# First mixture: the first of four weight groups multiplied plainly, token differences kept raw for two units

## The chip, the cores and the metric

The kernel runs on one core of one Trainium2 chip. The metric is the device time of one launch in microseconds. Shorter is better; each version is run several times and the median is told. TensorE multiplies into PSUM, ScalarE (ACT) and VectorE (DVE) read PSUM and SBUF, GpSimd (POOL) reads SBUF alone, and SyncE (SP) issues nearly all transfers between SBUF and DRAM.

## What is computed

Retention attention, then a dense mixture ("first mixture"), then a mixture of eight experts whose gate is balanced over tokens and experts ("second mixture"). All of it is float32.

```python
scores = scale * np.matmul(q, k.transpose(0, 1, 3, 2))
attn = np.matmul(scores * Dmat[None], v)               # 4 x 8 heads x 576 x 64
x = attn.transpose(0, 2, 1, 3).reshape(2304, 512)
h = x @ w_in                                           # w_in 512 x 2048: first mixture
x = (h * (1.0 / (1.0 + np.exp(-1.702 * h)))) @ w_out   # w_out 2048 x 512
...                                                    # P: gate of x, eight rounds of row and column sums
for e in range(8):
    out += P[:, e:e + 1] * (np.maximum(x @ w1[e], 0.0) @ w2[e])
```

The factors of the first mixture come in as 64-bit floats, seen as pairs of 32-bit words.

## The kernel before

**Exact products from two parts.** A float32 operand is split into a high part (a copy on ScalarE rounded to the matmul type float32r) and a low part (operand less high part, on VectorE or GpSimd). One product takes three matmuls: high by high, high by low, low by high.

**First mixture.** The 2048 inner columns are four groups of 512 (`G1`), the 2304 tokens three passes of 768 (`NPASS`), two halves `t` of `N` = 384 tokens each. One group and one pass make a unit; there are 12, units 0 to 2 with group 0, units 3 to 5 with group 1, and so on. A unit computes h for the two halves `h` of the group's columns, gates it (`gated`: two steps on ScalarE, then the low part, kept in `lows` until the next matmuls are issued) and multiplies by the group's part of `w_out` (`out_part`), whose result `out_done` copies into `xacc` (group 0, ScalarE) or adds to it (later groups, VectorE). In each half h comes by a scheme of seven products (`unit_step`, 0 to 6) instead of eight: weights AK, AL, BL and the sums S1 to S4, tokens X1K, X1L, X2L and the differences T1 to T4. So operands have to be made: sums of weights on GpSimd, differences of tokens on VectorE, and a high and a low part of each.

**Where the operands live.** `wi[0]` and `wi[1]` hold the seven weight operands of the two halves, `wo[0]` the split part of `w_out`. The tokens of a unit lie in seven of the 12 slots of `ring`; in units 0 to 2 they are made (`token_zero` during attention, `token_unit`) and put to `token_store`, from where `load_token` brings them for later groups. The differences overwrite blocks of `xacc`, the same blocks that `out_done` of the unit fills later.

**Weights.** 64-bit pieces of 128 x 256 arrive by `load_piece`; `read_piece` makes float32 of one in five steps on VectorE and one on ScalarE. Group 0's are joined by `add_piece` and split straight into `wi` by `direct_tasks`. For groups 1 to 3, and for the first two expert weights, `staged_tasks` splits each operand into a small buffer in `wo[1]` (`stage`), one or two of them, puts it to `sub_store` (`first_store`), and `load_sub` loads it into `wi` at the change of groups. `split_out` and `put_out` do the like for `w_out`, `load_out` loads it.

**Order.** All of it is in an order written by hand. After each slot (six matmuls; 30 slots to a unit) `run` issues the side work that `plan` holds for the slot; `place_tasks` spreads a list over a stretch of slots. Every engine, and SP's queue, works through its instructions in that order, and an instruction that waits holds those behind it. During attention (16 pairs of heads and batches) the same is done by `weave`, `settle` and the lists `prep` and `tok`.

Of the kernel before, what the change touches and what calls it, by code (L numbers as in the profile page):

```python
# [21 lines left out]
def retention_moe_kernel(  # L22
# [48 lines left out]
    ring = [keep.tile([P, 7 * 4 * N], F32R, name="ring0")]  # L71
    wi = [keep.tile([P, 14 * QF], F32R, name="wi0")]
# [129 lines left out]

    def split_out(g, i, h):
# [30 lines left out]
    def sums_of(r1, box):  # L234
# [19 lines left out]
        def src(o):  # L254
            if o in (S1, S3, S2, S4):
                return box["s"][:, (o - S1) % 2]
            return half(*{AK: (0, 0), AL: (0, 1), BL: (1, 1)}[o])

        return sums, src, half

    def direct_tasks(r1, w):


        box = {}
        sums, src, half = sums_of(r1, box)

        def whole(what):
# [1728 lines left out]
```

## Time and profile before

| what | us |
|---|---|
| median of 3 runs | 2004.01 (2003.08 to 2008.91) |
| the profiled execution, its time | 1998.25 |
| its span, first to last instruction | 1996.5 |
| attention ends, unit 0 begins | 84.58 |
| first mixture, units 0 to 11 | 464.77 |
| second mixture begins | 549.35 |
| TensorE busy | 1915.4 (96%) |
| VectorE, GpSimd, ScalarE busy | 1470.8, 1337.4, 749.8 |

The times of the middle rows are places in the profiled execution; the unit boundaries are the first matmul of each unit. A busy TensorE is one with a matmul in its pipe; where it was held, the idle time before an instruction is told with what ended it.

### The profile page before, as it was taken

Reading aid. Unit: us, or ns where it says so; the run is one execution under the profiler, and the core shown is the slowest. Engines: PE = TensorE matmul, PEld = TensorE weight load, DVE = VectorE, ACT = ScalarE, POOL = GpSimd, SP = SyncE. Lnnn points to the kernel's source line nnn. Section 1 sums busy time; section 2 is a strip of 40 time slices with the busy share of each in tenths; the row PEclk is TensorE's granted clock in tenths of the full one; section 3 lists DMA queues with packets and bytes.
Section 4 is the critical chain, followed back from the end, with each engine's and each line's share of the span. In section 5 each row is a group of like instructions: output and inputs, shape, how many; then the busy total and the mean of one; then the engine's idle time right before and its main releaser. Section 6 shows DMA issues by size and latency. Waiting matters only on the chain.

```text
span 1996.5 us, 33594 instructions
## 1 busy us (share of the span) xinstructions
PE 1915.4 (96%) x11431; PEld 1833.4 (92%) x11431; DVE 1470.8 (74%) x2454; ACT 749.8 (38%) x1600; POOL 1337.4 (67%) x1347
## 2 busy tenths in 40 slices
PE   9687798999999999999999999999999999999998
PEld 7577797888989889999999999999999999999998
DVE  6866456664678777777666888888777887777788
ACT  4544333334345444444443322222224222222462
POOL 5765233332168888888866777777777777777777
PEclk9989999999999999999999999999999999999999
DMA  9278968787368888888888777877778788777774
GB/s 392 103 290 307 337 233 288 287 290 295 133 239 300 296 300 301 297 310 316 303 294 272 254 272 247 272 254 260 261 255 269 255 288 263 258 261 253 270 245 169
DMA packets 246025, 538.42 MB, mean 270 GB/s; under 512 B 35168, under 2 KB 89184, under 8 KB 245088
## 3 DMA queue, kind: packets, MB, share of 16 engines
q1 hardware_dynamic: 232208, 534.62, 76.7%
q10 hardware_dynamic: 13648, 1.67, 0.5%
q8 instruction: 91, 1.49, 0.3%
q14 instruction: 78, 0.64, 0.1%
HBM read 380.15 MB, written 156.06 MB: 269 GB/s over the span
## 4 chain that ended last, share of the span: by engine, by line
PE 72%; DMA 10%; DVE 7%; POOL 5%; issue 3%; ACT 2%; SPq 0%; POOLq 0%; DVEq 0%; ACTq 0%
PE ps_p L1707 20%; PE ps_y L1337 13%; PE ps_z L1337 9%; PE ps_x L1337 9%; PE ps_m L1367 8%; PE ps_m L1261 4%; DMA sub<-wo 4%; PE ps_p L1719 3%; DMA second<-mix 2%; DMA r<-in_w_dram 1%; PE ps_y L1191 1%; DVE acc L1382 1%; DMA wo<-out 1%; PE ps_x L1191 1%; PE ps_z L1191 1%
## 5 line engine op out<-in xcount | busy, mean ns | idle before, releaser
L1731 DVE TENSOR_TENSOR acc<-ps_p,acc 128x768 f32<-128x768 f32 x420 | 399.9, 952 | 114.6 <-PE ps_p L1707 104.6
L1707 PE MATMUL ps_p<-wo,wi 128*128 128x384 f32 x2352 | 470.9, 334 | 0.1
L1707 PEld LDWEIGHTS ps_p<-wo,wi 128*128 128x128 f32 x2352 | 413.1, 188 | 0.8 <-issue 0.6
L1337 PE MATMUL ps_y<-ring,wi 128*128 128x384 f32 x1728 | 342.2, 335 | 0.0
L1590 POOL TENSOR_TENSOR wo<-u,wo 128x384 fp32r<-128x384 f32 x190 | 194.4, 1023 | 180.8 <-ACT wo L1589 180.8
L1337 PEld LDWEIGHTS ps_y<-ring,wi 128*128 128x128 f32 x1728 | 302.9, 188 | 3.4 <-issue 0.5
L1367 PE MATMUL ps_m<-wo,wo 128*128 128x512 f32 x1152 | 269.5, 391 | 0.2 <-DVE acc L1378 0.2
L1367 PEld LDWEIGHTS ps_m<-wo,wo 128*128 128x128 f32 x1152 | 215.0, 188 | 44.3 <-DVE acc L1382 0.7
L1589 ACT ACTIVATE wo<-u 128x384 fp32r<-128x384 f32 x191 | 100.4, 526 | 390.0 <-POOL u L1593 255.0
L1337 PE MATMUL ps_z<-ring,wi 128*128 128x384 f32 x1152 | 231.6, 335 | 2.5 <-DVE wo L1351 2.5
L1337 PE MATMUL ps_x<-ring,wi 128*128 128x384 f32 x1152 | 230.7, 334 | 0.0
L1337 PEld LDWEIGHTS ps_z<-ring,wi 128*128 128x128 f32 x1152 | 201.6, 188 | 4.4 <-DVE wo L1351 4.1
L1337 PEld LDWEIGHTS ps_x<-ring,wi 128*128 128x128 f32 x1152 | 201.9, 188 | 0.0
L1590 POOL TENSOR_TENSOR wo<-r,wo 128x384 fp32r<-128x384 f32 x127 | 132.2, 1041 | 22.8 <-ACT wo L1589 22.4
L1590 POOL TENSOR_TENSOR wo<-p,wo 128x384 fp32r<-128x384 f32 x127 | 136.3, 1073 | 5.5 <-ACT wo L1589 5.1
L1382 DVE SCALAR_TENSOR_TENSOR acc<-ps_m,pr,acc 128x512 f32<-128x512 f32 x168 | 123.7, 744 | 19.4 <-PE ps_m L1367 19.0
L1261 PE MATMUL ps_m<-g,wo 128*128 128x384 f32 x576 | 112.2, 348 | 22.5 <-DMA wo<-out 10.0
L1261 PEld LDWEIGHTS ps_m<-g,wo 128*128 128x128 f32 x576 | 104.4, 196 | 27.2 <-DMA wo<-out 11.2
L1589 ACT ACTIVATE wo<-p 128x384 fp32r<-128x384 f32 x127 | 65.9, 519 | 146.3 <-POOL p L1593 142.1
L1261 PE MATMUL ps_m<-wo,wo 128*128 128x384 f32 x576 | 104.0, 338 | 4.2 <-DVE acc L1275 4.2
L1261 PEld LDWEIGHTS ps_m<-wo,wo 128*128 128x128 f32 x576 | 101.4, 190 | 5.1 <-DVE acc L1275 5.1
L889 POOL TENSOR_TENSOR wi<-s,wi 128x512 fp32r<-128x512 f32 x60 | 78.4, 1306 | 39.8 <-ACT wi L882 39.2
(203 smaller groups left out, 3189.9 us busy)
## 6 DMA issues: line engine op xcount, KB each, us to landing
wi<-second SPq DMA_DIRECT2D x189, 512.0 KB, 5.1
wi<-first SPq DMA_DIRECT2D x135, 512.0 KB, 5.1
wi<-first SPq DMA_DIRECT2D x192, 256.0 KB, 4.8
ring<-token SPq DMA_DIRECT2D x63, 768.0 KB, 8.3
first<-wi SPq DMA_DIRECT2D x90, 512.0 KB, 3.7
r<-in_w_dram SPq DMA_DIRECT2D x64, 512.0 KB, 5.6
second<-wo SPq DMA_DIRECT2D x32, 512.0 KB, 3.1
second<-wt SPq DMA_DIRECT2D x64, 256.0 KB, 5.3
```

Source lines behind the costliest of these rows:

```text
L889: nc.gpsimd.tensor_tensor(out=wl[:, ks], in0=t[:, ks], in1=r32(wh[:, ks]), op=ALU.subtract)
L1191: nc.tensor.matmul(out=t[:, 0:N], lhsT=ops[:, w, hw, c], rhs=x[:, hx, c], start=begin and c == 0 and i == 0, stop=end and c == 1 and i == ...
L1261: nc.tensor.matmul(out=pd[:, 0:N], lhsT=w_out_of[:, d, hw, f], rhs=gs[t][:, f, hg], start=first and f == fs[0] and k == 0, stop=last and f ...
L1337: nc.tensor.matmul(out=t[:, 0:N], lhsT=w[:, o, hw, c], rhs=xq(q, x, hx, c), start=begin and c == 0 and i == 0, stop=end and c == 1 and i == 2,
L1367: nc.tensor.matmul(out=t, lhsT=x[:, is_], rhs=w[:, h, f], start=f == 0 and k == 0, stop=f == 1 and k == 2,)
L1382: nc.vector.scalar_tensor_tensor(out=oa, in0=tv, scalar=pr[:, ti, e : e + 1], in1=oa, op0=ALU.mult, op1=ALU.add)
L1589: nc.scalar.activation(out=h, in_=src, func=ACTF.Copy)
L1590: eng.tensor_tensor(out=l, in0=src, in1=r32(h), op=ALU.subtract)
L1707: nc.tensor.matmul(out=places[:, j], lhsT=w[:, hw, j * P : (j + 1) * P], rhs=a, start=k == 0, stop=k == 2,)
L1719: nc.tensor.matmul(out=t[:, j * QF : (j + 1) * QF], lhsT=a[:, js], rhs=w[:, hw], start=k == 0, stop=k == 2,)
L1731: nc.vector.tensor_tensor(out=e, in0=done, in1=e, op=ALU.add)
```

## The change

Units 0 to 2 compute h plainly: eight tiles (`h`, block `b`, token half `t`) of 12 matmuls each, on unsplit blocks of weights and tokens, in `plain_unit`. They have 32 slots. For that the eight input pieces of group 0 are split directly into four places of each `wi` (`split_in`), during attention; the tokens are split into four slots of the ring per pass (`plain_hi`, `plain_lo`; pass 0 from PSUM in attention, passes 1 and 2 in the unit before). In these units VectorE still makes the differences in `xacc`, but they are put raw to `diff_store` (`keep_diff`); two units later `load_token` loads one into half a slot, and `split_token` splits it there (two steps on ScalarE, two on GpSimd) and keeps it for groups 2 and 3. The undifferenced operands are kept as they are (`keep_plain_token`), and two stay in place for unit 3.

The staging of input weights goes. Of a later group one half waits as float32 in SBUF and the other in `half_store` (512 KB); in the last unit of the group before, behind its last use of `wi[0]` and of `wi[1]`, both are split directly into `wi` (`direct_tasks`). The first two expert weights are done likewise in unit 11. `put_out` has two buffers in turn. `load_out` moves forward, and the order of the output tiles in units 3 to 11 changes so that the first half of `wo` is done earlier. Token loads get fixed slots of a unit instead of the place behind the last use. In the second mixture two stores of first-layer weights are added and one PSUM bank is taken from another set.

```diff
-    ring = [keep.tile([P, 7 * 4 * N], F32R, name="ring0")]
-    wi = [keep.tile([P, 14 * QF], F32R, name="wi0")]
+    ring = [keep.tile([P, 4 * 4 * N], F32R, name="ring0")]
+    wi = [keep.tile([P, 14 * QF], F32R, name=f"wi{h}") for h in range(2)]
...
+    def split_in(g, i, h):
+        t, rest = [x.rearrange("p (b f) -> p b f", b=2) for x in raws.pop((g, i, h))]
+        l, c = divmod(i, 2)
+        wh, wl = [ops_of(wi[h])[:, l : l + 3 : 2, k, c] for k in range(2)]
+        nc.scalar.activation(out=wh, in_=t, func=ACTF.Copy)
+        nc.gpsimd.tensor_tensor(out=t, in0=t, in1=r32(wh), op=ALU.subtract)
+        nc.gpsimd.tensor_tensor(out=wl, in0=t, in1=rest, op=ALU.add)
...
-    def load_sub(g, h, o, n):
-        a, b = 2 * o * QF, 2 * (o + n) * QF
-        src = sub_store[g, h] if g < G1 else first_store[h]
-        nc.sync.dma_start(out=r32(wi[h][:, a:b]), in_=src[:, a:b])
...
+        if u < 2 * NPASS and o in DIFFS:
+            t = ring_slot(i)[:, 2 * N : 4 * N]
+            nc.sync.dma_start(out=r32(t), in_=diff_store[q][o])
...
+        return [lambda: hi(0), lambda: hi(1), lambda: lo(0), lambda: lo(1), keep]
...
+    def keep_diff(q, o):
+        l, t = DIFFS[o][2]
+        src = xacc[:, 2 * l : 2 * l + 2, q * PT + t * N : q * PT + (t + 1) * N]
+        nc.sync.dma_start(out=diff_store[q][o].rearrange("p (c n) -> p c n", c=2), in_=src)
...
-    place_tasks(direct_tasks(lambda: r1s[0, 1], ops_of(wi[1])), 0, 8)
-    place_tasks(piece_tasks(KF, False), 2, 17)
-    token_unit(1, 3, 22, 29)
-    token_unit(2, 33, 53, 59)
-    SPAN = {1: (22, 98), 2: (104, 186), 3: (192, 276)}
...
+        for k, o in enumerate((X1K, X1L, X2L)):
+            at(a + (1, 4, 7)[k], lambda q=q, o=o: keep_plain_token(q, o))
+        for k, o in enumerate((T1, T3, T2, T4)):
+            for c in range(2):
+                at(a + (2,6,13,21)[k] + c, lambda q=q, o=o, c=c: raw_diff(q, o, c, V))
+            at(a + (2,6,13,21)[k] + 3, lambda q=q, o=o: keep_diff(q, o))
+        if q < NPASS - 1:
+            for k, x in enumerate(XS):
+                at(a + 4 + 3 * k, lambda q=q, x=x: plain_hi(q + 1, *x))
+                at(a + 6 + 3 * k, lambda q=q, x=x: plain_lo(q + 1, *x, G))
...
+            for t, x in zip(split_token(i, G), (10, 11, 12, 14, 17)):
+                at(b + x, t)
+    place_tasks(piece_tasks(len(loads) + len(flight) - 16 * (G1 - 1), False), 0, 20)
+    SPAN = {1: (24, 70, 98), 2: (104, 161, 188), 3: (194, 251, 278)}
...
+        place_tasks(direct_tasks(lambda g=g: r1s[g, 0], ops_of(wi[0])), u + 8, u + 19)
+        at(u + 19, lambda g=g: load_half(g))
+        place_tasks(direct_tasks(lambda g=g: r1s[g, 1], ops_of(wi[1])), u + 23 + more, u + 34 + more)
+        at(u + 23 + more, lambda g=g: load_out(g, 0, 2))
+        at(u + 39 + more, lambda g=g: load_out(g, 2, 2))
...
+        for ds in ((0, 1), (2, 3)):
+            for t in (1, 0):
```

The order of instructions at three places. VectorE at the start of unit 0, before (`L1228` to `L1248` combine products, `L1213` is a gated low part, the rest are pieces):

```order
L1228 TENSOR_TENSOR u_1491<-ps_y,p_1480 128x384
L1234 TENSOR_TENSOR p_1501<-ps_z,p_1480 128x384
L154 TENSOR_SCALAR bits<-raw_1260 128x256
L163 SCALAR_TENSOR_TENSOR ca<-raw_1260,bits 128x256
L169 SCALAR_TENSOR_TENSOR ca<-cs,ca 128x256
L175 TENSOR_SCALAR bits<-ca 128x256
L1242 TENSOR_TENSOR p_1501<-ps_y,p_1501 128x384
L1213 TENSOR_TENSOR wo_1468<-ps_y,wo_1468 128x384
L181 SCALAR_TENSOR_TENSOR cs<-raw_1260,bits 128x256
L1248 TENSOR_TENSOR ps_z<-ps_z,u_1491 128x384
```

and after (`L357` is a difference, `L1168` a gated low part):

```order
L159 TENSOR_SCALAR bits<-raw_1112 128x256
L168 SCALAR_TENSOR_TENSOR ca<-raw_1112,bits 128x256
L174 SCALAR_TENSOR_TENSOR ca<-cs,ca 128x256
L180 TENSOR_SCALAR bits<-ca 128x256
L1168 TENSOR_TENSOR g_1450<-ps_x,g_1450 128x384
L357 TENSOR_TENSOR acc<-acc 128x384
L186 SCALAR_TENSOR_TENSOR cs<-raw_1112,bits 128x256
L357 TENSOR_TENSOR acc<-acc 128x384
```

The combining steps are gone and two differences stand early in the unit, between the steps of the pieces.

SP's queue in the last unit of group 0, before (`sub` is the store of split weights, `wo_1468` the buffer they are staged in):

```order
L341 DMA ring_1467<-token_166 128x1536
L318 DMA sub_156<-wo_1468 128x512
L232 DMA wi_73<-sub_155 128x1024
L318 DMA sub_156<-wo_1468 128x512
L232 DMA wi_73<-sub_155 128x1024
L318 DMA sub_156<-wo_1468 128x512
L232 DMA wi_73<-sub_155 128x1024
L232 DMA wi_73<-sub_155 128x512
```

and after (`diff` and `token` are the stores of tokens, `half` the float32 half, `out` the split part of `w_out`, `wo_75` its tile):

```order
L325 DMA ring_1445<-diff_172 128x768
L244 DMA out_161<-wo_1446 128x2x128 x2
L224 DMA r_2477<-half_157 128x1024
L325 DMA ring_1445<-diff_173 128x768
L142 DMA raw_2487<-in_w_in_dram 128x512
L328 DMA ring_1445<-token_186 128x1536
L362 DMA diff_184<-acc 256x1x384
L244 DMA out_161<-wo_1446 128x2x128 x2
L248 DMA wo_75<-out_161 128x2048
```

Stores and loads of split weights are replaced by one load of a half; the load of output weights stands in this unit.

ScalarE and GpSimd in the same unit, before (ScalarE first; `L304` is a high part into the staging buffer, `L1211`, `L1212` the gate, `L311` a low part into the buffer, `L250` a sum):

```order
L304 ACTIVATE wo_1468<-r_2308 128x256
L1211 ACTIVATE ps_x<-ps_x 128x384
L1212 ACTIVATE g_1472<-ps_x 128x384
L1211 ACTIVATE ps_z<-ps_z 128x384
L1212 ACTIVATE g_1472<-ps_z 128x384
L304 ACTIVATE wo_1468<-s 128x256
L1211 ACTIVATE ps_y<-ps_y 128x384
L1212 ACTIVATE wo_1468<-ps_y 128x384
L304 ACTIVATE wo_1468<-s 128x256
```

```order
L250 TENSOR_TENSOR s<-r_2308 128x256
L311 TENSOR_TENSOR wo_1468<-r_2308,wo_1468 128x256
L250 TENSOR_TENSOR s<-r_2308 128x256
L311 TENSOR_TENSOR wo_1468<-s,wo_1468 128x256 x2
L250 TENSOR_TENSOR s<-s,r_2308 128x256
L311 TENSOR_TENSOR wo_1468<-r_2308,wo_1468 128x256
```

and after (`L286` a high part into `wi`, `L271` a sum, `L293` a low part into `wi`, `L236` and `L237` a piece of `w_out`):

```order
L1167 ACTIVATE g_1450<-ps_x 128x384
L235 ACTIVATE wo_1446<-ca 128x256
L286 ACTIVATE wi_73<-r_2180 128x2x256
L1166 ACTIVATE ps_z<-ps_z 128x384
L1167 ACTIVATE wo_1446<-ps_z 128x384
L286 ACTIVATE wi_73<-r_2180 128x256
L286 ACTIVATE wi_73<-s 128x2x256
L1166 ACTIVATE ps_y<-ps_y 128x384
```

```order
L271 TENSOR_TENSOR s<-r_2180 128x256 x2
L236 TENSOR_TENSOR ca<-ca,wo_1446 128x256
L237 TENSOR_TENSOR wo_1446<-ca,cs 128x256
L293 TENSOR_TENSOR wi_73<-r_2180,wi_73 128x2x256
L293 TENSOR_TENSOR wi_73<-s,wi_73 128x2x256
L271 TENSOR_TENSOR s<-s,r_2180 128x256
L271 TENSOR_TENSOR s<-r_2180,s 128x256
```

The same splits now write the weight tile that the next unit reads, and no store stands between them.

## Rows read from the trace of the kernel before

**Rows 1.** Busy time by unit: stretch, length, engines (instructions), clock, DMA share, GB/s.

```profile
84.58:132.81 48.23, 36.37 (x185) 34.65 (x181) 33.40 (x64) 25.30 (x57) 31.69 (x35) 0.89 0.53 198
132.81:177.07 44.26, 35.11 (x182) 34.15 (x181) 26.84 (x51) 22.25 (x54) 27.37 (x31) 0.92 0.85 320
177.07:216.14 39.07, 32.88 (x181) 30.96 (x181) 19.08 (x44) 16.65 (x40) 17.19 (x23) 1.00 0.91 327
216.14:264.21 48.07, 35.36 (x182) 34.22 (x181) 28.91 (x66) 14.49 (x34) 14.75 (x19) 0.89 0.78 285
...
333.42:377.71 44.29, 35.97 (x182) 34.01 (x181) 28.44 (x64) 13.61 (x33) 14.64 (x19) 0.92 0.82 305
...
444.13:483.78 39.65, 34.14 (x181) 32.40 (x181) 18.94 (x40) 12.63 (x29) 10.52 (x14) 0.96 0.86 323
483.78:515.21 31.43, 31.43 (x182) 31.16 (x181) 16.48 (x31) 13.82 (x32) 12.29 (x17) 1.00 0.46 168
515.21:549.35 34.14, 34.14 (x214) 32.11 (x213) 22.30 (x43) 13.16 (x29) 2.49 (x3) 1.00 0.38 139
sum 464.77, PE 403.77 PEld 387.96 DVE 278.78 ACT 182.36 POOL 175.67; mean PE 33.65 PEld 32.33 DVE 23.23 ACT 15.20 POOL 14.64
```

**Rows 2.** TensorE's waits in the first mixture: total, times, longest (us).

```profile
PE ps_m L1261 <- DMA wo<-out: 10.0, 3, 7.8
PE ps_x L1191 <- DMA wi<-sub: 9.1, 3, 4.0
...
PE ps_y L1191 <- ACT wi L278: 6.9, 1, 6.9
...
PE ps_m L1261 <- ACT acc L1273: 5.5, 2, 4.7
```

**Rows 3.** Timeline of ScalarE and TensorE: start, length, instruction, [idle before, releaser].

```profile
162.49 0.42 ACT L304 ACTIVATE wo<-r 128x256 fp32r<-128x256 f32 x1 [6.67 <-DMA sub<-wo]
...
165.06 3.85 PE L1261 MATMUL ps_m<-g,wo 128*128 128x384 f32 x12 [4.68 <-ACT acc L1273]
...
249.90 6.15 PE L1261 MATMUL ps_m<-g,wo 128*128 128x384 f32 x24 [7.77 <-DMA wo<-out]
```

**Rows 4.** Timeline of VectorE in attention: last score step of five pairs.

```profile
29.16 0.22 DVE L469 TENSOR_TENSOR ret<-ps_end,tabs 128x64 f32<-128x64 f32 x1
...
35.68 0.22 DVE L469 TENSOR_TENSOR ret<-ps_end,tabs 128x64 f32<-128x64 f32 x1
...
47.31 0.22 DVE L469 TENSOR_TENSOR ret<-ps_end,tabs 128x64 f32<-128x64 f32 x1
...
55.52 0.22 DVE L469 TENSOR_TENSOR ret<-ps_end,tabs 128x64 f32<-128x64 f32 x1
...
78.23 0.22 DVE L469 TENSOR_TENSOR ret<-ps_end,tabs 128x64 f32<-128x64 f32 x1
```

**Rows 5.** GpSimd's groups in attention: count, busy, mean ns, idle before.

```profile
L429 POOL TENSOR_TENSOR qs<-kq,tabs 128x448 f32<-128x448 f32 x15 | 18.9, 1263 | 10.8 <-DMA tabs<-in_tab_dram 9.1 <-PE ps_avt L518 0.8 <-POOL vs L418 0.7
...
L418 POOL TENSOR_TENSOR vs<-aux,vt 128x512 f32<-128x512 f32 x14 | 15.3, 1090 | 13.0 <-PE ps_stt L481 5.6 <-DMA aux<-in_vk_dram 5.0 <-PE ps_avt L518 1.3
...
L213 POOL TENSOR_TENSOR ca<-ca,wo 128x256 f32<-128x256 f32 x4 | 3.4, 856 | 0.3 <-ACT wo L212 0.3
L214 POOL TENSOR_TENSOR wo<-ca,cs 128x256 fp32r<-128x256 f32 x4 | 3.0, 742 | 0.3
```

**Rows 6.** Timeline: differences on VectorE beside a GpSimd multiply and alone.

```profile
35.81 1.45 DVE L359 TENSOR_TENSOR acc<-acc 128x384 f32<-128x384 f32 x1
...
35.71 1.14 POOL L429 TENSOR_TENSOR qs<-kq,tabs 128x448 f32<-128x448 f32 x1
...
128.76 0.55 DVE L359 TENSOR_TENSOR acc<-acc 128x384 f32<-128x384 f32 x1
```

**Rows 7.** DMA issues of the first mixture: count, KB each, us to landing.

```profile
token<-ring SPq DMA_DIRECT2D x21, 768.0 KB, 5.1
sub<-wo SPq DMA_DIRECT2D x42, 256.0 KB, 3.5
```

More of the change, by code (lines that the diff above doesn't have):

```diff
@@ L252, in sums, with src @@
             return go
[L254 to L267, printed above, removed]
+        def src(what):
             if what == "a":
@@ L334, in pieces @@
         second = [[(g, KD + f, h) for f in range(KF)] for h in range(2)]
-        return first[0] + second[0] + first[1] + second[1]
+        if g == 0:
+            return first[0] + first[1] + second[0] + second[1]
+        return first[1] + second[0] + first[0] + second[1]
+    DIFFS = {
+        T1: ((0, 1), (0, 0), (0, 0)),
+        T3: ((1, 1), (0, 1), (0, 1)),
+        T2: ((1, 1), (0, 0), (1, 1)),
+        T4: ((1, 0), (1, 1), (1, 0)),
+    }
+    PLAIN = {X1K: (0, 0), X1L: (1, 0), X2L: (1, 1)}
@@ L337, in load_token @@
+    IN_PLACE = (21, 24)
     def load_token(i):
         u, o = divmod(i, 7)
[L339 to L354 removed]
@@ L357, in raw_diff, with keep_plain_token @@
+    def keep_plain_token(q, o):
+        l, t = PLAIN[o]
+        for h in range(2):
+            d = token_store[q][:, 4 * o * N : 4 * (o + 1) * N]
+            d = d.rearrange("p (h n) -> p h n", h=2)[:, h]
+            s = xp(q, l, t, h, slice(0, 2)).rearrange("p c n -> p (c n)")
+            nc.sync.dma_start(out=d, in_=r32(s))
     def raw_diff(q, o, c, eng):
@@ L666, in retention_moe_kernel @@
         weave(len(woven))
-        if p == NP:
-            settle()
-            ask()
-            read(3)
-            weave(len(woven))
-        for _ in range(3):
-            if prep:
-                prep.pop(0)()
-        for _ in range(6 if p >= 13 else 3):
-            if tok:
-                tok.pop(0)()
-    while prep:
-        prep.pop(0)()
-    while tok:
-        tok.pop(0)()
-    while decoded:
-        settle()
+    assert not decoded and not woven
     att.close()
@@ L1127, in retention_moe_kernel @@
     raw2 = []
-    def token_unit(q, a, b, c):
-        now = []
-        def one(what, *args):
-            return [lambda i=i: what(q, *args[:1], i, *args[1:]) for i in range(2)]
-        def op(o):
-            ts = one(raw_diff, o, nc.vector) if o in DIFFS else []
-            return ts + one(raw_hi, o) + one(raw_lo, o, nc.gpsimd) + [lambda: keep_token(7 * q + o)]
-        for o in (X1K, T1, X1L, T3, T2):
-            now += op(o)
-        place_tasks(now, a, b)
-        place_tasks(op(X2L) + op(T4), b, c)
@@ new lines, in retention_moe_kernel @@
+    FIRST = {22: 38, 23: 41, 25: 50, 26: 53, 27: 55, 28: 58, 29: 81, 30: 84, 31: 87, 32: 90}
+    for n in range(NPASS, NUNIT):
+        for o, i in enumerate((8, 10, 13, 17, 21, 25, 29)):
+            FIRST[7 * n + o + NSLOT] = start_of(n) + i
+    for i, b in FIRST.items():
+        at(b, lambda i=i: load_token(i))
+        u, o = divmod(i, 7)
+        if u < 2 * NPASS and o in DIFFS:
+            for t, x in zip(split_token(i, G), (10, 11, 12, 14, 17)):
+                at(b + x, t)
+    place_tasks(piece_tasks(len(loads) + len(flight) - 16 * (G1 - 1), False), 0, 20)
@@ L1300, in retention_moe_kernel @@
         i = 18
-        for t, ds in ((1, (2, 3)), (0, range(KD))):
+        for t, ds in ((0, (0, 1)), (1, (2, 3)), (0, (2, 3))):
             for d in ds:
```

235 lines of the change are left out of this document (112 added, 123 removed).

## The prediction

> **What bounds the kernel now.** I read the busy shares by unit of the first mixture first, since the change lies there [rows 1]. A unit is 84 + 96 matmuls of 384 columns; unit 10 shows them with nothing in the way: 31.43 us, TensorE busy throughout, granted clock 1.00. The twelve units together take 464.77 us, that is 88 us over 12 x 31.43. The surplus is uneven: units 0 to 2 have 131.6 us, and the first unit of each later group 48.07, 44.29 and 39.65; unit 11 also holds the gate matmuls. The four units whose rows are not shown share 464.77 - 329.14 = 135.6 us, 33.9 each. From unit 11 on TensorE is nearly always busy, so the second mixture is taken as unchanged, and only the time before it can move.
>
> The waits of TensorE say which stalls these are [rows 2]: loads of staged weights (wo<-out 10.0, wi<-sub 9.1), the split of group 0's second half (ACT wi 6.9), and copies on ScalarE (5.5). That last one has a cause further back [rows 3]: at 162.49 ScalarE had stood 6.67 us because its staging buffer was still being stored; its queue is in order, so the copy that frees a PSUM bank came late and TensorE stood 4.68 us. A long stall costs twice: behind the 7.77 us one, 24 matmuls took 6.15 us, against 24 x 0.175 = 4.2 us at unit 10's pace; that unit's granted clock is 0.89 in the mean, so part of it ran at 1.2 GHz and not at 2.4.
>
> Attention before it is bound by VectorE once token work begins. Five ends of a pair's last score step [rows 4]: two pairs without differences take 6.5 us, two with 11.6, two without 8.2, three with 22.7.
>
> **The change, part by part.**
>
> *Plain units, added matmuls.* In three units the input product is done plainly, eight tiles of 12 matmuls, instead of by seven products of 6 for each half: 96 + 96 matmuls instead of 84 + 96. At 31.43/180 = 0.1746 us, 36 more cost 6.3 us, so a plain unit's floor is 33.5.
>
> *Attention.* Differences and their splits of pass 0 (16 VectorE steps) and the seven-operand splits of the first weights leave; four more high and low parts, and two GpSimd steps per piece instead of one, come in. A pair then costs GpSimd 1.09 + 1.26 + 0.86 + 0.74 = 3.95 us [rows 5], above the 3.3 us that a pair free of token work took. The nine pairs of rows 4 go from 49.1 us to 9 x 3.95 = 35.5, 13.5 less. GpSimd waits for ScalarE inside each pair; I allow 0.3 us each and take **-11**; bounds -14 and -4 (the second if loads or those waits hold a pair at 5 us).
>
> *Start of the mixture.* All eight input pieces are split directly during attention, so the 6.9 us wait has nothing left to wait for. What is late next is VectorE. Unit 0 of before shows 64 VectorE instructions in 33.40 us, 0.52 each. The new unit 0 has nine pieces of five instructions, eight differences and eight low parts, 61 x 0.52 = 31.8 us of 33.5; unit 1 has 56 (29.2 us), unit 2 41 (21.4). They are not even: counted by slot of six matmuls (1.05 us), VectorE is some 4.5 us behind at slot 14 of unit 0, where the output product at slot 17 wants the seventh low part. That, the table load and a spell at the lower clock: **unit 0 38.5, unit 1 36, unit 2 34.5**, 109.0 against 131.6. Bounds: 100.5 (floor) and 131 (as now).
>
> First what a row shows [rows 6]: one and the same difference takes 0.55 us with GpSimd idle and 1.45 us when a GpSimd multiply (35.71) is under way. The Trainium skill (GPSIMD Engine Reference, 1. Specifications) says that GpSimd's SBUF interfaces are shared with VectorE and contend with its instructions of two SBUF inputs. It speaks against this change, which puts 24 differences beside GpSimd's low parts; if each met one, 24 x 0.9 = 22 us of VectorE would be added to the shorter time, and the sum would end near 1954. The mean of 0.52 above already holds eight differences under like company, so I keep it.
>
> *Stores of differences.* 12 stores of 384 KB; between 3.5 us (256 KB) and 5.1 (768 KB) by [rows 7]. On ScalarE's queue the output copies over the same token blocks wait for them, with everything of ScalarE behind. They are issued 5 to 16 slots before those copies, and three PSUM banks (6 us) plus four tiles of the next unit (8 us) stand behind a late one. I cost them at 0, bounds 0 and 1 us each.
>
> *Staging gone.* The 42 stores and 24 loads of split input weights vanish, and ScalarE's waits for them. In their place the group's last unit splits both halves straight into the weight tiles, the second from one 512 KB load. GpSimd has the longest chain: four sums, four low parts per half, beside four pieces and four token low parts. Unit 2 of after has about 34 GpSimd instructions from slot 0 on; at 31.69/35 = 0.905 us (unit 0 [rows 1]) that is 31 of 33.5 us. The last low part falls near slot 7 or 8 of unit 3, and product S2 of the second half wants it at slot 8. I take 2 us of stall and 0.6 of clock: **unit 3 34.0**; bounds 31.4 and 44. Groups 2 and 3 carry no token work there: **33 each** for units 6 and 9. The output weights are loaded 20 slots before use rather than 9, so 10.0 us of waiting goes; the four middle units lose ScalarE's standing but keep VectorE's pieces: **32.4 each**, between 31.4 and 33.9. Units 10 and 11 stay.
>
> *Token operands of passes 3 to 5.* 12 splits of two ScalarE and two GpSimd steps move two units later, ten slots behind their load; free unless GpSimd is late, which the term for unit 3 holds.
>
> *Sum of the mixture.* 109.0 + 34 + 33 + 33 + 4 x 32.4 + 31.4 + 34.1 = 404.1, against 464.8: **-60.7**. With attention -71.7. The profiled execution took 1998.25 (span 1996.5): 1926.5. The median of the runs shown lies 5.8 above that execution, so I say **1932**.
>
> **The rivals.**
>
> 1. *VectorE full in the plain units.* If differences meet GpSimd and pieces wait for ScalarE as before, units 0 to 2 keep their 131.6 us: +22.6, 1955. For: 31.8 of 33.5 us is hardly any room. Against: ScalarE no longer stands on staging stores there, and pieces have until slot 24.
> 2. *Attention stays.* Loads or GpSimd hold the pair near 5 us; -4 rather than -11, or nothing: 1939 to 1943.
> 3. *Hand-over late.* Direct splits end 8 us too late at four changes of weights; 8 us and 2 of clock each, less the 5.8 us already held: +34, 1966. For: GpSimd at 31 of 33.5 us. Against: only the first change has token work beside it.
> 4. *Slower.* ScalarE stands at each of the 12 output copies that overwrite a difference, as it stood 6.67 us at 162.49. If every one stops TensorE in full, 12 x 6.67 = 80 us eats the gain: 2012. It decides where a store lands more than some 14 us after it is due; the row shows stands of that size, but half is hidden by the banks and tiles named.
> 5. *Better.* All terms at their floor: mixture 385.8, attention -14: 1911.
>
> That staging might remain in another form is excluded by the order: no sub store is left.
>
> **How the numbers follow.** Forecast 0.60 (1916 to 1947 on its own), rival 1 0.14, rival 2 0.13, rival 3 0.06, rival 4 0.04, rival 5 0.03. The range for 8 in 10, 1913 to 1959, takes in rivals 1 and 2. A measurement of this kernel tells some 0.3% (6 us) from no change. All cases but rival 4 are faster by more: 0.96; of rival 4's 0.04, 0.01 falls within 0.3% and 0.03 is slower.
>
> **What would show it.** By unit: 38, 36, 34.5, 34, then 31.4 to 33, and second mixture starting near 478 instead of 549. Attention ending near 74 instead of 84.6. No TensorE wait on wi<-sub or ACT wi; wo<-out under 2 us. ScalarE's waits on stores under 10 us in all. Wrong if VectorE's lag in unit 0 exceeds 8 us, if TensorE waits for GpSimd wi at units 3, 6, 9 by more than 5 us, or if output copies wait for diff stores.

## The result, and the profile after

The changed kernel takes 1914.47 us (median of four runs, 1913.68 to 1915.53) against 2003.55 us before: ratio 0.9552, 95% interval 0.9532 to 0.9571. The profiled execution took 1915.53 us, with a span of 1913.7. The prediction said 1932, within 1913 to 1959: the sign and the range hold, and the time lies 17.5 us below the forecast. That is below the 1916 to 1947 that the prediction gave its own forecast, and 3.5 us above its fifth rival, "Better" (1911, all terms at their floor).

| stretch | before | after | forecast |
|---|---|---|---|
| attention ends | 84.58 | 71.91 | 73.6 |
| units 0, 1, 2 | 48.23, 44.26, 39.07 | 33.44, 33.28, 37.24 | 38.5, 36, 34.5 |
| units 3, 6, 9 | 48.07, 44.29, 39.65 | 37.23, 32.77, 31.20 | 34, 33, 33 |
| units 4, 5, 7, 8 together | 135.63 | 124.94 | 129.6 |
| units 10, 11 | 31.43, 34.14 | 31.20, 34.14 | 31.4, 34.1 |
| first mixture | 464.77 | 395.44 | 404.1 |
| second mixture | 1447.15 | 1446.35 | as before |

The first view is the busy time by unit of the kernel after (stretch, length, then busy time and instruction count of TensorE, its weight loads, VectorE, ScalarE and GpSimd, then granted clock, DMA share, GB/s); its lines answer to [rows 1].

```profile
71.91:105.35 33.44, 33.44 (x196) 33.44 (x193) 29.09 (x60) 20.81 (x48) 19.44 (x22) 1.00 0.53 178
105.35:138.63 33.28, 33.28 (x193) 33.28 (x193) 24.31 (x53) 20.14 (x47) 19.21 (x21) 1.00 0.78 264
138.63:175.87 37.24, 34.91 (x194) 33.08 (x194) 23.85 (x47) 18.54 (x44) 25.54 (x28) 1.00 0.99 361
175.87:213.10 37.23, 33.34 (x181) 32.70 (x181) 22.00 (x49) 16.21 (x37) 17.05 (x20) 0.95 0.74 259
...
275.57:308.34 32.77, 31.99 (x181) 31.10 (x181) 23.92 (x54) 12.14 (x28) 12.13 (x15) 1.00 0.81 285
...
370.81:402.01 31.20, 31.20 (x181) 31.20 (x181) 13.41 (x25) 9.28 (x19) 6.37 (x7) 1.00 0.72 279
402.01:433.21 31.20, 31.20 (x181) 31.20 (x181) 16.21 (x31) 10.76 (x23) 1.01 (x1) 1.00 0.25 85
433.21:467.35 34.14, 34.14 (x213) 32.11 (x213) 24.30 (x43) 16.38 (x35) 17.58 (x17) 1.00 0.27 92
sum 395.44, PE 388.45 PEld 382.76 DVE 270.25 ACT 179.34 POOL 176.09; mean PE 32.37 PEld 31.90 DVE 22.52 ACT 14.95 POOL 14.67
```

Units 0 and 1 have TensorE busy from end to end, although each has 12 matmuls more: 33.28 us for 192 matmuls is just under the forecast floor of 33.5. Two units stand out, 2 and 3, with some 4 and 6 us above their floors; of the later units all are at or near 31.2 but unit 6 (32.77) and unit 11, which holds the gate matmuls too. The granted clock, 0.89 in units 0 and 3 of before, is 1.00 but for unit 3's 0.95. Of the 69.3 us that the mixture lost, 54.0 were time in which TensorE had nothing in its pipe (464.77 - 403.77 = 61.0 before, 395.44 - 388.45 = 7.0 now), and 15.3 were busy time, although 36 matmuls were added: with the long waits most of the slow matmuls behind them went too.

The next view is who waited for whom in the same stretch (total, times, longest, us): all five rows of TensorE's own waits, and below them three of ScalarE's.

```profile
PE ps_x L1149 <- ACT ps_y L1166: 3.4, 2, 2.6
PE ps_x L1149 <- ACT p L1178: 1.3, 1, 1.3
PE ps_m L1216 <- ACT acc L1228: 1.1, 1, 1.1
PE ps_z L1244 <- DVE wo L1168: 1.0, 1, 1.0
PE ps_y L1244 <- DVE wo L1168: 0.2, 1, 0.2
...
ACT acc L1228 <- DMA diff<-acc: 14.3, 4, 6.1
...
ACT ring L334 <- DMA ring<-diff: 8.2, 3, 3.5
...
ACT wo L235 <- DMA out<-wo: 1.1, 1, 1.1
```

Where [rows 2] has 10.0 us for output weights, 9.1 for staged weights and 6.9 for the late split, TensorE now waits 7.0 us in all, and for no load at all. ScalarE's stands on staging stores [rows 3] are gone but for 1.1 us. In their place it stood 14.3 us, in four stands, on the new stores of token differences (`diff<-acc`). Two of the prediction's signs failed here: its last sign of being wrong, "if output copies wait for diff stores", came true, and ScalarE's waits on stores, which were to stay under 10 us in all, are 15.4. It is the mechanism of the fourth rival; the 80 us of that rival was a price in time, and in time the stores cost 8.5 us (below).

The longest stand, 6.06 us at 143.62, falls early in unit 2: the copies and gates behind it on ScalarE come late, and with them VectorE's low parts, for which TensorE waits in that unit (the rows `DVE wo L1168`, 1.2 us). What another of these stands does is told by the timelines of SP's queue, ScalarE, GpSimd and TensorE around the start of unit 3 (start, length, instruction, [idle before, releaser]).

```profile
169.65 0.52 SPq L362 DMA_DIRECT2D diff<-acc  x1
...
177.47 0.49 ACT L1228 ACTIVATE acc<-ps_m 128x384 f32<-128x384 f32 x1 [3.62 <-DMA diff<-acc]
...
178.79 0.41 ACT L235 ACTIVATE wo<-ca 128x256 fp32r<-128x256 f32 x1
...
179.27 0.73 POOL L236 TENSOR_TENSOR ca<-ca,wo 128x256 f32<-128x256 f32 x1 [4.39 <-DMA wo<-out]
...
184.63 0.72 POOL L271 TENSOR_TENSOR s<-r,s 128x256 f32<-128x256 f32 x1
185.39 0.63 ACT L286 ACTIVATE wi<-s 128x512 fp32r<-128x512 f32 x1 [5.02 <-POOL s L271]
185.93 0.47 ACT L1166 ACTIVATE ps_y<-ps_x 128x384 f32<-128x384 f32 x1
...
186.45 1.40 PE L1149 MATMUL ps_x<-ring,wi 128*128 128x384 f32 x6 [2.62 <-ACT ps_y L1166]
187.65 3.77 PE L1149 MATMUL ps_y<-ring,wi 128*128 128x384 f32 x12
```

The last difference store of unit 2 is issued at 169.65, and ScalarE's copy over that block can start 7.8 us later, having stood 3.62 us. Behind it in ScalarE's order is a piece of `w_out` (178.79), on whose high part GpSimd's next step waits: it starts at 179.27, 0.07 us after 178.79 + 0.41 (the row names the load of `wo`; ScalarE's step is the event that fits, and the run without the stores names it for the same step). Behind that are GpSimd's sums of weights; ScalarE's next high part stands 5.02 us on the last of them, with a gate behind it, and TensorE stops for 2.62. Then twelve matmuls take 3.77 us instead of 2.24. Not all of this is the stand's. In the run without the stores (below) the same chain is there: ScalarE stands 4.35 us on the same sum and TensorE 0.74 (behind the removed line its line numbers are one lower).

```profile
171.63 0.73 POOL L236 TENSOR_TENSOR ca<-ca,wo 128x256 f32<-128x256 f32 x1 [1.88 <-ACT wo L235]
...
177.79 0.63 ACT L286 ACTIVATE wi<-s 128x512 fp32r<-128x512 f32 x1 [4.35 <-POOL s L271]
...
178.85 1.31 PE L1148 MATMUL ps_x<-ring,wi 128*128 128x384 f32 x6 [0.74 <-ACT ps_y L1165]
```

But there GpSimd's step at its head starts 0.1 us ahead of unit 3 (171.71), in the changed kernel 3.4 us behind its start (175.87). The stand of 3.6 us has crossed three engines almost whole.

### The profile page after: what moved, and what is told of

The parts are those of the page before. It is cut to its first block, busy times and chain, and to the rows that moved or that the text cites. A ratio compares the mean times of both kernels' runs of the same rounds, so it can differ in the third digit from the quotient of the medians.

```text
span 1913.7 us, 33421 instructions
## 1 busy us (share of the span) xinstructions
PE 1896.8 (99%) x11467; PEld 1827.0 (95%) x11467; DVE 1449.7 (76%) x2423; ACT 743.8 (39%) x1578; POOL 1331.7 (70%) x1324
## 4 chain that ended last, share of the span: by engine, by line
PE 89%; DMA 4%; DVE 4%; POOL 2%; ACT 1%; issue 1%; SPq 0%; DVEq 0%; ACTq 0%; POOLq 0%
PE ps_p L1698 21%; PE ps_y L1327 14%; PE ps_m L1357 11%; PE ps_x L1327 10%; PE ps_z L1327 10%; PE ps_m L1216 8%; PE ps_p L1710 3%; PE ps_y L1149 3%; PE ps_x L1149 2%; PE ps_z L1149 2%; DMA r<-in_w_dram 1%; PE ps_y L1244 1%; PE ps_avt L509 1%; PE ps_ts L441 1%; DMA diff<-acc 1%; DVE acc L1372 1%
## 5 line engine op out<-in xcount | busy, mean ns | idle before, releaser
L1216 PE MATMUL ps_m<-g,wo 128*128 128x384 f32 x576 | 105.5, 334 | 0.0
L1216 PEld LDWEIGHTS ps_m<-g,wo 128*128 128x128 f32 x576 | 100.3, 188 | 0.3 <-DVE g L1168 0.3
```

The source lines that it names most:

```text
L1216: nc.tensor.matmul(out=pd[:, 0:N], lhsT=w_out_of[:, d, hw, f], rhs=gs[t][:, f, hg], start=first and f == fs[0] and k == 0, stop=last and f ...
```

## The experiments

**Which of the two units' excess is the stores?** Four runs on the changed kernel.

The differences earlier in all three plain units:

```diff
-                at(a + (2,6,13,21)[k] + c, lambda q=q, o=o, c=c: raw_diff(q, o, c, V))
-            at(a + (2,6,13,21)[k] + 3, lambda q=q, o=o: keep_diff(q, o))
+                at(a + (2,6,10,14)[k] + c, lambda q=q, o=o, c=c: raw_diff(q, o, c, V))
+            at(a + (2,6,10,14)[k] + 3, lambda q=q, o=o: keep_diff(q, o))
```

> The same as the changed kernel, but the four differences of a plain unit stand at slots 2, 6, 10 and 14 instead of 2, 6, 13 and 21 (and their stores three slots behind each), so that the last store is issued seven slots earlier. Theory A (late stores): the 8 us by which units 2 and 3 exceed 33.3 and 31.2 come from ScalarE standing on difference stores (14.3 us in four stands); with more time in front of the copies the stands fall under 4 us, units 2 and 3 take 33.3 to 34.5 and 31.2 to 32.5, and the time is 1905 to 1909. Theory B (bytes): unit 2 moves 13.4 MB at a DMA share of 0.99, and the bytes stay the same, so units 2 and 3 stay within 1 us of 37.2 and the time at 1914. Theory C (GpSimd's chain of splits, as the prediction had it for unit 3): unit 2 falls to 34, unit 3 stays at 36 to 37, time 1911.

1908.64 us (1907.09 to 1909.76; ratio to before 0.9527, 0.9511 to 0.9543). The first four units:

```profile
71.59:106.00 34.41, 33.72 (x196) 33.38 (x193) 28.16 (x60) 20.80 (x48) 19.60 (x22) 1.00 0.50 174
106.00:139.28 33.28, 33.28 (x193) 33.28 (x193) 25.36 (x53) 20.91 (x49) 20.15 (x22) 1.00 0.83 281
139.28:173.49 34.21, 33.60 (x193) 33.19 (x193) 25.16 (x46) 20.01 (x46) 25.65 (x28) 1.00 1.02 377
173.49:206.44 32.95, 32.14 (x181) 31.09 (x181) 21.98 (x49) 14.70 (x33) 17.08 (x20) 1.00 0.81 289
```

Units 2 and 3 give back 7.3 us, and ScalarE's standing on difference stores falls from 14.3 us to 1.9. The bytes are the same and unit 2 moves them faster (377 GB/s against 361), so theory B falls: the full DMA share in unit 2 was no limit at 361 GB/s. Theory C is right in a remainder only: unit 3 stays 1.7 us above 31.2. Unit 0 lost 1.0 us, which no theory had; it is taken up below.

The differences later (slots 5, 11, 17, 23):

> The differences of a plain unit at slots 5, 11, 17 and 23 instead of 2, 6, 13 and 21, their stores three slots behind. The copies over the same blocks begin at slots 17, 21, 25 and 29, so that a store that lands 4 to 6 us after its issue comes 1 to 3 us late for every copy. Theory A: ScalarE stands on six to twelve stores, 3 to 6 us each, and TensorE loses 1 to 3 us in each: 1922 to 1940. Theory B (bytes) and theory C (GpSimd): within 3 us of 1914.

1923.69 us (1920.06 to 1924.8), as theory A said. ScalarE's stands on the stores, as its waits show, nearly double, and TensorE's wait for its copies goes from 1.1 to 5.3 us:

```profile
PE ps_m L1216 <- ACT acc L1228: 5.3, 3, 3.2
PE ps_x L1149 <- ACT p L1178: 3.6, 1, 3.6
...
ACT acc L1228 <- DMA diff<-acc: 27.1, 6, 6.5
```

Units 0 to 3 took 35.89, 34.27, 42.18 and 38.63 us: with 12.8 us more of standing these four are 9.8 us longer.

The stores left out, the loads pointed at other stored tokens:

```diff
-            at(a + (2,6,13,21)[k] + 3, lambda q=q, o=o: keep_diff(q, o))
-            nc.sync.dma_start(out=r32(t), in_=diff_store[q][o])
+            nc.sync.dma_start(out=r32(t), in_=token_store[q][:, 0 : 2 * N])
```

> The 12 stores of differences are left out; the loads that bring them back two units later read the first half of the stored operand X1K instead, which is as large (so the products use other tokens). Price of the stores, bytes and waits together. Theory A: ScalarE never stands on a store, units 2 and 3 take 33.3 to 34 and 31.2 to 32.5, time 1905 to 1909, the same as with the early differences. Theory B: unit 2 has 11.9 instead of 13.4 MB, 33 us at 361 GB/s; unit 3 stays at 36 to 37; time 1909 to 1911. Theory C: unit 2 falls by 1 to 3 us, unit 3 stays; 1911.

1905.96 us (1905.69 to 1907.08): the 12 stores cost 8.5 us in all, nothing in units 0 and 1 (33.42, 33.28), 4.0 in unit 2 (33.28) and 4.3 in unit 3 (32.92). What is left in unit 3 is not the stores'.

The stores on ScalarE's queue instead of SP's (`nc.sync` becomes `nc.scalar` in `keep_diff`):

> The 12 stores of differences are issued on ScalarE's queue instead of SP's, at the same slots. In the changed kernel SP issued the stores of unit 2 up to 9 us behind their slot, because a piece load ahead of them waited for its buffer. Theory A with SP's order as the cause: the stores leave within 2 us of the difference, the stands fall under 5 us in all, time 1906 to 1910. Theory B (bytes; a store in unit 2 takes 5.8 us to land wherever it is issued): stands stay above 10 us, time 1912 to 1916. Against both: ScalarE itself waits for VectorE's difference before it can issue, which could cost some us: 1915 to 1920.

1909.56 us (1907.54 to 1912.08). Unit 2 is at 33.31; ScalarE stood 0.2 us on the stores. So in unit 2 it is their place in SP's queue that made them late, with the same bytes. Unit 3 took 35.03 all the same, 2.1 us more than without the stores: ScalarE stood 5.06 us on GpSimd's sum again, and TensorE 1.96. This is not the stand on a store. The rows name a second way in, the load of the float32 half:

```profile
167.84 0.63 ACT L286 ACTIVATE wi<-r 128x512 fp32r<-128x512 f32 x1 [2.21 <-DMA r<-half]
```

This step starts 3.3 us ahead of unit 3 (171.18), in the changed kernel 4.9 and without the stores 5.7, and the chain of splits hangs on it. Why the load was late here, no run shows.

**How near is VectorE in the plain units?** The next pass's low parts on VectorE instead of GpSimd (`plain_lo(q + 1, *x, V)`):

> The eight low parts of the next pass's tokens that units 0 and 1 make on GpSimd are made on VectorE. It asks how near VectorE is to being the bound there. Theory D (VectorE full, the prediction's lag): 29.1 us of unit 0 plus 8 x 0.55 = 33.5 us of 33.4, low parts of the gate come late, unit 0 takes 36 to 39, unit 1 34 to 35, time 1917 to 1921. Theory E (relief): without GpSimd's steps beside them the differences fall from 0.85 and 0.60 us in the mean to 0.55, so VectorE has 31 us in unit 0 and 28.5 in unit 1; both stay at 33.3 to 34, time 1914 to 1916.

1915.75 us (one run). Units 0 and 1:

```profile
71.78:106.26 34.48, 33.69 (x197) 33.37 (x194) 30.67 (x68) 20.82 (x48) 11.97 (x14) 1.00 0.50 175
106.26:139.54 33.28, 33.28 (x194) 33.28 (x194) 27.82 (x59) 19.94 (x47) 14.73 (x16) 1.00 0.77 255
```

Eight instructions more cost VectorE only 1.6 us in unit 0 (30.67 against 29.09), as theory E said (it gave 31): the differences beside it got shorter. Unit 0 still grew by 1.0 us, more than theory E allowed (33.3 to 34) and far less than theory D (36 to 39), so its room on VectorE ends about here.

A third of the plain tiles' matmuls left out:

```diff
-                    for j, (hw, hx) in enumerate(((0, 0), (0, 1), (1, 0))):
+                    for j, (hw, hx) in ((0, (0, 0)), (2, (1, 0))):
```

> The products high weight by low token are left out of the plain tiles of units 0 to 2 (32 of 96 matmuls in each unit; the result lacks that part). Each matmul is 0.1733 us in units 0 and 1. If TensorE alone is the bound: units 0 and 1 fall by 5.5 us each to 27.8, all that the matmuls cost. If VectorE is next: unit 0 ends at 29.5 to 32 (29.1 us of work), unit 1 near 28 (24.3 us). Unit 2, which is held by stores, falls by less than 5.5 in either case.

1915.72 us (one run). The 32 matmuls of a unit, 5.5 us of TensorE, buy 0.3 us in unit 0 and 2.6 in unit 1:

```profile
71.24:104.34 33.10, 30.41 (x164) 29.28 (x161) 29.05 (x60) 20.51 (x48) 19.39 (x22) 0.95 0.51 180
104.34:135.02 30.68, 28.52 (x161) 27.55 (x161) 23.75 (x51) 19.58 (x47) 18.19 (x20) 1.00 0.79 281
```

Both expectations were too low. VectorE's 29.05 us are not spread evenly over the unit, and TensorE meets the late ones. The timeline of the shortened unit 0 shows it; the seventh low part (`L1168`, 88.89) comes 17.65 us after the unit's start:

```profile
83.71 2.93 PE L1244 MATMUL ps_y<-ring,wi 128*128 128x384 f32 x8 [2.02 <-DVE wo L1168]
...
88.89 0.55 DVE L1168 TENSOR_TENSOR g<-ps_y,g 128x384 fp32r<-128x384 f32 x1
...
89.50 2.52 PE L1216 MATMUL ps_m<-g,wo 128*128 128x384 f32 x13 [0.64 <-DVE g L1168]
...
146.50 2.93 PE L1244 MATMUL ps_x<-ring,wi 128*128 128x384 f32 x8 [5.76 <-DVE g L1168]
```

In the full kernel the same step comes at 89.83, 17.92 us after its unit's start: VectorE runs at the same pace whether TensorE has 96 or 64 matmuls to do. Unit 0 is thus bound by both engines at once: TensorE fills it, and VectorE alone would hold it at 33.1.

The last row lies in unit 2, which grew to 40.03 us instead of falling, against the expectation; with 96 matmuls fewer the whole kernel is no faster than the changed one. TensorE came to the unit's fifth tile sooner, ScalarE stood 7.51 us on a difference store instead of 6.06, and TensorE waited 5.76 us for a low part behind that stand.

**The loads of output weights and the two buffers.** The loads moved back to where they stood:

```diff
-        at(u + 23 + more, lambda g=g: load_out(g, 0, 2))
-        at(u + 39 + more, lambda g=g: load_out(g, 2, 2))
+        at(u + 34 + more, lambda g=g: load_out(g, 0, 2))
+        at(u + 41 + more, lambda g=g: load_out(g, 2, 2))
```

> The two loads of output weights at each change of group stand where they stood in the kernel before, four and eleven slots into the new unit, instead of nine slots ahead of its start and nine slots into it. Theory F (the advance pays): the load of 1 MB takes 6.3 to 8.9 us to land and the first use is nine slots later, so TensorE waits 0.5 to 4 us at each of three changes and loses some clock: 3 to 10 us, 1918 to 1925. Rival: the waits of the kernel before came from the staging stores and loads on the same queue, which are gone: within 2 us of 1914.

1916.92 us (one run), 2.4 above the changed kernel, which a single run can't tell from no change. TensorE waited for no output weights at any of the three changes; units 6 and 9 took 32.64 and 31.20, as in the changed kernel, and the waits of units 2 and 3, which took 2.8 us more, are on VectorE, ScalarE and GpSimd. The rival holds as far as the place of the loads goes: with the queue as it now is (and the new order of output tiles, which stayed), nine slots are enough, so the advance alone isn't what removed the 10.0 us of [rows 2].

One staging buffer for the pieces of `w_out` (`stage[0]` in `split_out` and `put_out`):

> The split pieces of w_out share one staging buffer instead of two in turn. Theory G (the buffer's turn counts, as the standing of 76 us on staging stores did in the kernel before): ScalarE waits for two thirds of 24 stores, 2 to 5 us each, 40 to 70 us in all, and TensorE loses 5 to 15 us in units 1 to 8: 1920 to 1930. Rival: with 1.5 to 4 us between two pieces the copies stay early enough and the banks hide the stands: within 2 us of 1914.

1922.31 us (one run): units 1, 4, 6 and 7 take 36.82, 32.38, 34.57 and 33.23 instead of 33.28, 31.26, 32.77 and 31.26. ScalarE's waits show why:

```profile
ACT wo L235 <- DMA out<-wo: 24.4, 8, 5.8
```

It stands on 8 of 24 pieces, not on two thirds. The mixture is 8.1 us longer for 23 us more of standing here; as the stands on difference stores fell from 14.3 to 9.9 us in this run, ScalarE stood some 19 us more in all, and about 0.4 of a stand comes through.

**What bounds attention?** GpSimd's second step of the eight input pieces left out, the low part made in one:

```diff
-        nc.gpsimd.tensor_tensor(out=t, in0=t, in1=r32(wh), op=ALU.subtract)
-        nc.gpsimd.tensor_tensor(out=wl, in0=t, in1=rest, op=ALU.add)
+        nc.gpsimd.tensor_tensor(out=wl, in0=t, in1=r32(wh), op=ALU.subtract)
```

> For the eight input pieces split in attention GpSimd has one step instead of two: the low part is the word less its high part, and the small rest of the 64-bit number is left out (the result lacks that). It asks what bounds attention in the changed kernel, where GpSimd has 14.4 and VectorE 13.9 us of work in the 15 us from 40 to 55, and a pair takes 4.1 us. GpSimd as the bound: each of the eight pairs loses 0.73 us, and VectorE's step beside it, 0.99 us in the mean with GpSimd busy and 0.42 without, shortens too; attention ends 5 to 7 us earlier, at 65 to 67, time 1908 to 1910. VectorE as the bound: at 69.5 to 71.5, time 1912 to 1915.

1911.96 us (one run). Attention ends at 70.09; in the eleven traces that leave it as it is (the changed kernel and ten variants) it ends between 71.15 and 71.91, 71.45 in the mean. Two rows of the changed kernel, a pair with little for VectorE and the nine pairs from the last score step at 30.68 to the one at 67.84, and then the same nine pairs of this run:

```profile
21.24:24.98 3.74, 3.74 (x74) 3.38 (x76) 1.52 (x4) 1.51 (x7) 3.10 (x4) 1.00 1.02 406
30.68:67.84 37.16, 36.56 (x652) 32.48 (x651) 35.61 (x82) 20.68 (x81) 33.63 (x36) 1.00 0.82 321
```

```profile
30.40:65.15 34.75, 34.31 (x636) 30.44 (x633) 33.58 (x82) 20.15 (x78) 26.85 (x27) 1.00 0.87 345
```

GpSimd drops from 33.63 to 26.85 us, VectorE stays full (96 and 97% of the stretch) with the same 82 steps, and the nine pairs get 2.4 us shorter, close to the 2.0 by which VectorE's steps do. Behind them 0.9 us is lost again (4.94 us to the end of attention against 4.07), so that 1.4 of 5.8 us come through. VectorE is the bound, and GpSimd acts on it mainly by making its steps longer. TensorE, which nobody named, has a matmul in its pipe nearly throughout as well; but at the pace of the first row (74 in 3.74 us) the 652 of the nine pairs would take 33 us, so by this estimate it bounds them only some 4 us below, and 2 to 3 us below in this run. No run leaves VectorE's steps out to test that.

**A better place for the differences.** Early in units 1 and 2 alone:

```diff
+                at(a + ((2,6,10,14) if q else (2,6,13,21))[k] + c, lambda q=q, o=o, c=c: raw_diff(q, o, c, V))
+            at(a + ((2,6,10,14) if q else (2,6,13,21))[k] + 3, lambda q=q, o=o: keep_diff(q, o))
```

> The early slots 2, 6, 10, 14 for the differences in units 1 and 2 alone; unit 0 keeps 2, 6, 13, 21. With early differences in all three units, unit 0 took 34.41 instead of 33.44, because VectorE there has no room ahead of slot 17. If so, unit 0 is 33.4 again, units 2 and 3 stay at 34.2 and 33.0, and the time is 1906 to 1908.5. If the loss in unit 0 came from elsewhere, unit 0 stays at 34.4 and the time at 1908.6.

1907.07 us (1905.78 to 1907.54; ratio to before 0.9528, 0.9514 to 0.9542). Units 0 to 3:

```profile
71.29:104.72 33.43, 33.43 (x196) 33.43 (x193) 29.10 (x60) 20.80 (x48) 19.45 (x22) 1.00 0.51 181
104.72:138.00 33.28, 33.28 (x193) 33.28 (x193) 25.87 (x55) 21.05 (x49) 20.90 (x23) 1.00 0.84 287
138.00:171.28 33.28, 33.28 (x193) 33.28 (x193) 23.89 (x45) 19.93 (x46) 25.24 (x27) 1.00 1.03 388
171.28:204.17 32.89, 32.12 (x181) 31.05 (x181) 21.97 (x49) 14.70 (x33) 17.07 (x20) 1.00 0.79 281
```

Unit 0 is back at its floor, so its 1.0 us in the first run was the place of the differences in VectorE's order (there the seventh low part ran at 90.53, 18.9 us after the unit's start, and TensorE waited 0.7 us for it). Unit 2 reaches the floor with its 13 MB at 388 GB/s. This version beats both kernels: 7.4 us below the changed one, their runs apart from each other and its mixture 8.7 us shorter, though the two intervals of the ratio overlap.

The same, and the last high and low part of the second half two slots later:

```diff
-        place_tasks(direct_tasks(lambda g=g: r1s[g, 1], ops_of(wi[1])), u + 23 + more, u + 34 + more)
+        ts = direct_tasks(lambda g=g: r1s[g, 1], ops_of(wi[1]))
+        place_tasks(ts[:10] + [None, None], u + 23 + more, u + 34 + more)
+        at(u + 36 + more, ts[10])
+        at(u + 36 + more, ts[11])
```

> As the run before it, and in the last unit of a group the high part of the sums S2 and S4 of the second half (ScalarE) and its low part (GpSimd) stand two slots later. In the early run ScalarE stood 4.4 us on GpSimd's sum ahead of that step, with a gate behind it, and TensorE waited 0.8 us and lost clock. If the stand is the rest of unit 3's and unit 6's surplus: unit 3 falls from 33.0 to 31.2 to 32, unit 6 from 32.3 to 31.2 to 31.8, time 1904 to 1906.5. If GpSimd's last low part is what is late, unit 3 stays or grows by up to 1.5 us, time 1907 to 1910.

1910.15 us (1909.78 to 1911.83): worse. Units 3, 6 and 9 take 33.76, 32.98 and 32.98 instead of 32.89, 32.35 and 31.20, and TensorE now waits for the splits themselves:

```profile
PE ps_y L1152 <- ACT wi L286: 2.3, 3, 1.3
PE ps_y L1152 <- POOL wi L293: 2.2, 3, 0.7
```

So the direct splits have less than two slots (2 us) of room at every change of weights. ScalarE's stand on the sum at unit 3 is gone in this run, and the time with it isn't: the remaining 1.7 us of unit 3 fit that chain of sums and splits, but no run has shortened the chain to show it, and a later place is no cure.

**One part of the change alone.** The kernel before without its 42 stores of staged input weights (`sub<-wo`):

```diff
             def go():
+                if any(store is x for x in sub_store.values()):
+                    return
...
-        src = sub_store[g, h] if g < G1 else first_store[h]
+        src = token_store[0] if g < G1 else first_store[h]
```

> The kernel before, without the 42 minus 14 ... that is without all stores of staged split weights of groups 1 to 3; their loads read stored tokens of the same size instead, so the products are of other numbers. One part of the change alone: ScalarE and GpSimd still split every operand, but no longer stand on the stores. If these stands (76.3 us on ScalarE in the kernel before) are what held the middle units and the changes of weights: units 4, 5, 7 and 8 fall from 33.9 in the mean to 32 to 32.7, units 1 and 2 lose 5 to 10 us, the rest 5, time 1975 to 1985. If the banks hid the stands and VectorE's work held the units: less than 6 us, 1997 to 2003.

1975.37 us (1973.7 to 1976.51; ratio to before 0.9872, 0.9856 to 0.9889). Four of its units, 0, 1, 3 and 4:

```profile
85.91:134.09 48.18, 36.50 (x184) 34.77 (x181) 33.37 (x64) 25.26 (x57) 31.64 (x35) 0.86 0.53 198
134.09:170.07 35.98, 32.42 (x181) 31.02 (x181) 29.00 (x52) 22.68 (x55) 29.03 (x32) 1.00 0.97 365
...
204.97:252.31 47.34, 36.82 (x181) 35.73 (x181) 28.59 (x65) 14.47 (x34) 14.35 (x19) 0.82 0.75 273
252.31:283.51 31.20, 31.20 (x181) 31.20 (x181) 19.82 (x43) 13.01 (x31) 10.42 (x14) 1.00 0.64 229
```

The mixture falls from 464.77 to 437.97 us. (All 42 are left out; the subtraction in the expectation is a slip.) Unit 1 gets 8.3 us, units 4, 5, 7 and 8 together 6.4; VectorE's work in them is as before (unit 4: 19.82 us, before 19.97), so the stores held unit 4, by ScalarE's standing or by their bytes (the DMA share of that unit was 0.73 before and is 0.64); VectorE's pieces didn't. Units 0 and 3 get next to nothing: unit 0 still has the 6.9 us of the late split, and in unit 3 TensorE still waits for reloads, 5.1 us for `wi` and 5.4 for output weights. ScalarE's stands fell by less than the 76.3 us of the staging stores, since those on pieces of `w_out` (`out<-wo`) rose from 15.2 to 26.6. So of the 69.3 us that the change takes from the mixture, the stores alone were 26.8. Direct splits in place of reloads and the plain first group with its early splits share the rest; the runs don't part them further.

## Why the prediction was right, and where its sizes were off

- **The offset (6.6 of the 17.5 us).** The sum was made against a profiled execution of 1998.25, and some 5.5 us were added for the median, which lay 5.8 above it. In the kernel after, the median lies 1.1 below the profiled execution. The difference was that execution's, not the kernel's: later runs of the kernel before scatter from 1998.4 to 2007.2.
- **Attention (1.7 us).** Forecast end 73.6, measured 71.91. The nine pairs took 4.13 us each (last score steps at 30.68 and 67.84) against 3.95 with 0.3 of waits. The size was right; the engine named was not. GpSimd's work was the price, but the run with less of it shows that VectorE sets the pace. That both engines need nearly 4 us for a pair is luck as far as the prediction goes.
- **Unit 0 (5.1 us) and unit 1 (2.7).** The term that failed is the 5 us for VectorE's lag, the table load and a lower clock. The lag is real: the seventh low part was due at slot 14, 86.5, and ran at 89.83, 3.3 us late against 4.5 forecast. But its first reader is among the last matmuls of slot 17, which ends at 71.91 + 18 x 1.04 = 90.6, so a lag of 3.3 us had some 4 us of cover (0.55 of it for the step itself), and the granted clock stayed 1.00. ScalarE's table load is there (1.28 us at 72.81), but TensorE did not stop for it. VectorE's 60 instructions averaged 0.485 us, not 0.52.
- **The rule on GpSimd and VectorE.** The 24 differences took 18.1 us where 24 x 0.55 is 13.2: they lost 4.9 us, not the 22 if each had met a GpSimd step. The Trainium skill (GPSIMD Engine Reference, 1. Specifications) holds that GpSimd shares its SBUF interfaces with VectorE and contends with steps of two SBUF inputs; the trace agrees in kind (0.55 to 1.44 us for one and the same step). Keeping the mean was the right choice. The run with the low parts on VectorE shows it from the other side: 16 differences fell from 11.6 to 10.3 us.
- **Units 2 and 3 (2.7 and 3.2 us too low).** For unit 3 GpSimd's chain was to cost 2.6 us; without any stores it costs 1.7, and moving its end by two slots makes TensorE wait. That step was about right, though not in its reasons: GpSimd had 28 steps and 25.5 us of work in unit 2, not 34 and 31, and TensorE waits not for the last low part but for a gate that stands on ScalarE behind the sum's high part. The step that failed is "I cost them at 0" for the difference stores: they cost 8.5 us, 0.7 each, within the bound of 1 us that was kept for them, and their sign of being wrong came true. The cover that I named, banks and tiles, hid most of each stand from the matmuls that wait for the bank; it didn't hide what else was queued on ScalarE: gates, and pieces, on which GpSimd's splits hang.
- **Units 4 to 9 (6.7 us).** The middle units were given 1.2 us above their floor for VectorE's pieces and have next to none: 31.2 throughout, although VectorE has more to do in unit 4 than before (23.78 against 19.97 us). Most of what those units lost before was the staging stores (6.4 of their 10.7 us go with the stores alone). Unit 9 likewise took 31.20 against 33.
- **Loads of output weights.** The forecast that their 10.0 us vanish holds, its reason doesn't: nine slots suffice in the queue as it now is.
- **The rivals.** VectorE full: nearly so, since that low part ended at 90.38 with its reader at some 90.6, but not over. Hand-over late: only 1.7 us in unit 3, 1.6 in unit 6, nothing in unit 9. Attention stays: no, it lost 12.7 us. Stores standing: the right mechanism at a small size. Better: nearest in time, since units 0, 1 and most later ones did reach their floors, while units 2 and 3 did not.
- **The sum.** It is right in part because its errors have both signs: 5.9 us too low in units 2 and 3, some 23 too high elsewhere, and more than a quarter of those is the offset.

## What to carry over

When the engine that bounds changes, ask for a late result not how late it is but which matmul reads it first: 3.3 us of lag were free behind 4 us of cover, and the next step that took a microsecond of it showed at once. A wait on an in-order engine is to be priced by all that is queued behind it on that engine, and by who waits for that, and a store that must land before an overwrite should be issued as soon as its data exist. An offset between one profiled execution and the median is not a property of the kernel.

## What the runs showed of the hardware

- A DMA share of 0.99 in a stretch is no sign of a limit: unit 2 moved 361 GB/s at 0.99 and 388 GB/s at 1.03 when the stores stood earlier.
- VectorE's step from two SBUF operands (`L174`, 128x256) took 0.99 us in the mean in attention beside GpSimd and 0.79 with a fifth less GpSimd work there (26.85 instead of 33.63 us in nine pairs); the same step took 0.41 to 0.42 us where GpSimd was idle (at 73.56, 79.05 and 83.22) and up to 1.26 beside it. Not every GpSimd step beside it counts: at 40.70 it took 0.42 us beside one.
